# Attention with a relative bias, then a feed-forward layer: a new order for batch 0, other places for the q and k copies, 28 instead of 32 FFN matmuls per head pair

## The chip, the cores and the metric

The kernel runs on one core of a Trainium2 chip. The time is the device time of one execution in microseconds (us). A core has five engines with a queue of instructions each, worked off in order: TensorE (matmuls; its weight loads overlap them), VectorE, ScalarE, GpSimd and SyncE. They wait for each other through semaphores. Matmuls write to PSUM, a small memory of eight banks; VectorE and ScalarE read them from there. Transfers between the chip's main memory and the on-chip SBUF are issued here by GpSimd (loads) and SyncE (stores, transposing copies).

## The reference

Eight batches of eight heads, 576 rows, head size 64. The bias depends on the distance of two rows alone (32 buckets, the last from distance 128 on). The output of the attention, laid out as 4608 tokens of 512 numbers, goes through two matrix products with a leaky ReLU between them.

```python
scores = scale * np.matmul(q, k.transpose(0, 1, 3, 2))
scores = scores + bias.transpose(2, 0, 1)[None, :, :, :]
attn = np.exp(scores - np.max(scores, axis=-1, keepdims=True))
attn = attn / (np.sum(attn, axis=-1, keepdims=True) + 1e-09)
x = np.matmul(attn, v)            # then (batch, row) x (head, d): 4608 x 512
h = x @ w_in                      # 512 -> 2048
out = np.maximum(0.01 * h, h) @ w_out
```

## The kernel before

**Pairs.** The unit of the attention is a pair of heads `n` of 32 (four pairs `p` per batch `b`). Its steps are functions:

- `pair_rows(n)` (VectorE): copies the rows of q and k of two heads next to each other (tile `pr`).
- `transpose_q(n)`, `transpose_k(n)`: bring q and k to the form with the head dimension on the partitions (`qt`, `kt`). Up to pair 9 TensorE transposes into PSUM, from pair 10 on SyncE's transposing copy does it three pairs ahead (`turn_by_dma`, tile `tu`); a copy on VectorE or ScalarE writes `qt` and `kt`, and `apart` adds a form of the last 64 rows for both heads.
- `qk_mm(n, u)`: the scores, transposed, in six parts: `u` = 0 to 3 are four blocks of 128 key rows against the first 512 query rows (tile `ps_s`, two buffers of two banks), `u` = 4 is these blocks against the last 64 query rows (`ps_q`), `u` = 5 the last 64 key rows (`ps_s`).
- `exp(n, u, ps)` (ScalarE) writes the exponentials to `at` and `at4`, two buffers each by the parity of `n`.
- `band(n, u)` (VectorE) multiplies the diagonal band of the exponentials by the exponential of the bias, taken from tables `hk` and `hk4`. These are made at the start: row `ub` from the bias table, written to memory, and read back shifted by one per partition.
- `av_tails(n)`, `av(n, 0)`, `av(n, 1)`: value products of the last 64 key rows, then of the first and the second head (tile `ps_o`, one buffer, two banks, shared with `ps_q`). A column of ones in v gives the sum. After each `av`, VectorE takes the reciprocal and divides into `opair`.
- `x_transposes(n)`: `opair` to `xT`, by TensorE and a VectorE copy up to pair 5, for the last pair too, and by SyncE between.

**FFN.** Nine tiles of 512 tokens. An in-piece is four matmuls 128x512 and one activation on ScalarE (16 per tile), an out-piece four matmuls of an accumulation of 16 (16 per tile); after every fourth out-piece VectorE copies `y` and SyncE stores it. `moe(k)` does up to `k` in-pieces, `moe_block()` four out-pieces, or in-pieces if no out-piece is ready. A token tile is ready when its batches are finished (`finished`), and the in-pieces are at most two tiles ahead of the out-pieces. What is left after pair 32's step is done in `moe_rest()`, the tail. Pieces take their PSUM banks from a pool of two (`ps_m`, tag "m"), shared with transposes and in the tail joined by others.

**Order.** It is written by hand: each engine's instructions run in the program's order. The start warms TensorE with matmuls on zeros (`spin`), then pairs 0 and 1 are scored in a loop of their own (lines 531 to 545), with value products of pair 0 behind it. From pair 2 on a loop (line 553) does in turn: scores 0 and 1 of pair `n`, the value products of pair `n - 1` with an in-piece behind each, scores 2, 3, 4, `x_transposes(n - 1)`, the first half of the block, score 5, the q and k transposes and copies of pair `n + 1` (from pair 5 on), the second half of the block, two in-pieces.

Of the kernel before, what the change touches and what calls it, by code (L numbers as in the profile page):

```python
# [11 lines left out]
BF16 = mybir.dt.bfloat16  # L12
# [6 lines left out]
def bucket_runs(n_buckets, max_distance, seq):  # L19

    half = n_buckets // 2
    n = np.arange(seq)
    lr = np.log(np.maximum(n, 1).astype(np.float32) / half) / np.log(max_distance / half)
    large = np.minimum(half + (lr * (half - 1)).astype(np.int32), n_buckets - 1)
    bucket = np.where(n < half, n, large)
    assert (bucket[max_distance:] == n_buckets - 1).all()
    runs = []
    for d in range(max_distance):
        u = int(bucket[d])
        if runs and runs[-1][0] == u:  # L30
            runs[-1][2] = d
        else:
            runs.append([u, d, d])
    return runs
# [3 lines left out]
def kernel(  # L38
# [10 lines left out]
    nc = tc.nc  # L49
# [132 lines left out]
    C0 = 2 * P - 1  # L182
    small = NB // 2
    nc.vector.tensor_copy(out=ub[:, C0 : C0 + small], in_=e8[:, 0:small])
    for u, lo, hi in bucket_runs(NB, BAND, S):
        if lo >= small:
            nc.vector.tensor_copy(
                out=ub[:, C0 + lo : C0 + hi + 1],
                in_=e8[:, u : u + 1].to_broadcast([H, hi - lo + 1]),
            )  # L190
    row = ub[:, :]
    nc.vector.tensor_copy(
        out=ub[:, C0 - BAND + 1 : C0],
# [5 lines left out]
    def load_hk(h0, h1):  # L199
        nc.sync.dma_start(  # L200
            out=hk[:, h0:h1, :],
            in_=bass.AP(tensor=udr, offset=h0 * UW, ap=[[1, P], [UW, h1 - h0], [1, BW]]),
        )

    load_hk(0, 2)
    for e in range(2):
        nc.sync.dma_start(
            out=hk4[e * SL : (e + 1) * SL, :, :],
            in_=bass.AP(tensor=udr, offset=e * UW + SL + P, ap=[[1, SL], [2 * UW, n_pairs], [1, P + SL]]),
        )  # L210
    load_hk(2, H)

    def mirrored(t, lo, hi):

# [49 lines left out]
    def turned_pair(n, j):  # L264

        if by_dma(n):
            return turned[n][:, j * NC : (j + 1) * NC, :].rearrange("p c r -> p r c")
        if n <= n_pairs:
            ps = ps_m_pool.tile([P, 8 * P], BF16, name="ps_t", tag="m")
        else:  # L270
            if j == 0:
                turned[n] = ps_o_pool.tile([P, 2, 8 * P], BF16, name="ps_tt", tag="o")
            ps = turned[n][:, j, :]
        for c in range(NC):
            nc.tensor.transpose(ps[:, c * RQ : (c + 1) * RQ], in_=prs[n][0:RQ, j, c, :],
                                identity=ident[0:RQ, 0:RQ])
        return ps[:, 0:S].rearrange("p (c r) -> p r c", c=NC)
# [7 lines left out]

    def transpose_q(n):
        qt = qts[n] = qt_pool.tile([P, S], BF16, name="qt")
        copy = nc.scalar.copy if n <= n_pairs and n != 1 else nc.vector.tensor_copy
        copy(out=qt[:, 0:S].rearrange("p (r c) -> p r c", c=NC), in_=turned_pair(n, 0))  # L289

    def transpose_k(n):
        kt = kts[n] = kts_[n % 2]
        nc.vector.tensor_copy(out=kt[:, 0:S].rearrange("p (r c) -> p r c", c=NC), in_=turned_pair(n, 1))  # L293
        apart(kt)

    def qk_mm(n, u):

        qt, kt = qts[n], kts[n]
        if u == NJ:
            ps = ps_o_pool.tile([P, 2, 512], FP32, name="ps_q", tag="o")  # L300
            for c in range(NJ):
                for e in range(2):
                    r = slice(e * D, (e + 1) * D)
                    nc.tensor.matmul(ps[:, e, c * SL : (c + 1) * SL], lhsT=kt[r, c * P : (c + 1) * P],
                                     rhs=qt[r, 512:S], start=True, stop=True)
            return ps
        ps = ps_s_pool.tile([P, 2, 512], FP32, name="ps_s")
        if u < NJ:
            for e in range(2):
                r = slice(e * D, (e + 1) * D)  # L310
                nc.tensor.matmul(ps[:, e, :], lhsT=kt[r, u * P : (u + 1) * P], rhs=qt[r, 0:512],  # L311
                                 start=True, stop=True)
        else:
            nc.tensor.matmul(ps[:, 0, :], lhsT=kt[:, S : S + P], rhs=qt[:, 0:512], start=True, stop=True)
            nc.tensor.matmul(ps[:, 1, 0:SL], lhsT=kt[:, S : S + P], rhs=qt[:, 512:S], start=True, stop=True)  # L315
        return ps
# [4 lines left out]
    def exp(n, u, ps):  # L321
        at, at4 = at_view(n), at4_[n % 2]
        if u < NJ:
            nc.scalar.activation(at[:, :, u, 0:512], ps, AF.Exp, scale=scale)  # L324
        elif u == NJ:
            nc.scalar.activation(at[:, :, :, 512:S],  # L326
                                 ps[:, :, 0 : NJ * SL].rearrange("p e (c i) -> p e c i", i=SL),
                                 AF.Exp, scale=scale)
        else:
            nc.scalar.activation(at4[:, 0:S], ps.rearrange("p e i -> p (e i)")[:, 0:S], AF.Exp, scale=scale)  # L330
# [166 lines left out]
    def spin(k):  # L497
        pw = ps_m_pool.tile([P, 512], FP32, name="ps_w", tag="m")
        for _ in range(k):
            nc.tensor.matmul(pw, lhsT=junk[:, 0:P], rhs=junk, start=True, stop=True)  # L500

    def bands(n):
        for u in range(NJ + 2):
            band(n, u)

    spin(11)

    pair_rows(0)
    transpose_k(0)
    transpose_q(0)  # L510
    spin(5)
    def begin(n):
        b, p = items[n]
        if n == 0:
            load_w_in(0)
            load_v(1, 0, H, False)
            load_w_in(1)
            load_w_out(0)
            load_w_out(1)
        elif 0 < b < B - 1:  # L520
            if p < 2:
                load_qk(b + 1, 4 * p, 4 * p + 4)
            if p > 0:
                load_v_part(b + 1, p - 1)
        if n + 1 < N and not by_dma(n + 1):
            pair_rows(n + 1)
        if n + AHEAD < N and by_dma(n + AHEAD):
            pair_rows(n + AHEAD)
            turn_by_dma(n + AHEAD)

    for n in range(2):
        begin(n)
        ps_a, ps_b = qk_mm(n, 0), qk_mm(n, 1)
        exp(n, 0, ps_a)
        exp(n, 1, ps_b)
        transpose_q(n + 1)
        spin(3)
        ps_a, ps_b, ps_c = qk_mm(n, 2), qk_mm(n, 3), qk_mm(n, 4)
        exp(n, 2, ps_a)
        exp(n, 3, ps_b)  # L540
        transpose_k(n + 1)
        spin(4 - n)
        ps_a = qk_mm(n, 5)
        exp(n, 4, ps_c)
        exp(n, 5, ps_a)
    bands(0)
    av_tails(0)
    av(0, 0)
    av(0, 1)
    x_transposes(0)  # L550
    bands(1)

    for n in range(2, N + 1):
        live = n < N
        early = n + 1 <= n_pairs
        if x_by_dma(n - 2):
            finished(n - 2)
        if live:
            begin(n)
            ps_a, ps_b = qk_mm(n, 0), qk_mm(n, 1)  # L560
            exp(n, 0, ps_a)
            exp(n, 1, ps_b)
        av_tails(n - 1)
        av(n - 1, 0)
        if live:
            band(n, 0)
        if early:
            transpose_q(n + 1)
        moe(1)
        av(n - 1, 1)  # L570
        if live:
            band(n, 1)
        if early:
            transpose_k(n + 1)
        moe(1)
        if live:
            ps_a, ps_b, ps_c = qk_mm(n, 2), qk_mm(n, 3), qk_mm(n, 4)
            exp(n, 2, ps_a)
            band(n, 2)
            exp(n, 3, ps_b)  # L580
            exp(n, 4, ps_c)
            band(n, 4)
        x_transposes(n - 1)
        if not x_by_dma(n - 1):
            finished(n - 1)
        block = moe_block()
        next(block)
        if live:
            ps_a = qk_mm(n, 5)
            exp(n, 5, ps_a)  # L590
            band(n, 5)
        if n + 1 < N and not early:
            transpose_q(n + 1)
            transpose_k(n + 1)
        next(block)
        moe(2)
    moe_rest()


# [28 lines left out]
```

## Time and profile before

| what | us |
|---|---|
| median of 3 runs (428.47 to 433.93) | 429.24 |
| the profiled execution | 429.74 |
| its span, first to last instruction | 428.0 |
| TensorE busy | 376.7 |
| ScalarE busy | 239.5 |
| VectorE busy | 200.2 |
| GpSimd busy | 67.8 |

The mean granted TensorE clock of the profiled execution is 0.976 of full speed. Matmuls are pipelined, and a matmul's shown end is modelled, so the distance of two starts says more than the shown duration. In the timeline rows the columns are start, duration, engine, line, operation, output <- inputs, form, count, and in brackets the idle time of the engine before it with what ended it. In the rows of waits they are who waited for whom, us in total, times, and the longest. A few per cent of the matmul records are missing, so counts such as x3 or x7 stand for 4 or 8.

### The profile page before, as it was taken

To read this page: it belongs to the slowest core of one execution; us is meant where nothing else is said; L and a number is where in the kernel's file an instruction comes from. 1 tells how busy PE (TensorE), PEld (TensorE's weight loads), DVE (VectorE), ACT (ScalarE), POOL (GpSimd) and SP (SyncE) were. 2 spreads that over 40 slices of the span, in tenths; PEclk is the share of its full clock that TensorE was granted. 3 is DMA by queue.
4 is the path that set the end of the run, shared out by engine and by line. 5 is a ranking of instruction groups with operands and counts; after the bars stand their busy time and mean duration, and the time that the engine had idled before them with its cause. 6 is when DMAs were issued, how large, how long until landed. Compare 5 with 4: busy or idle time off the path is not lost.

```text
span 428.0 us, 8434 instructions
## 1 busy us (share of the span) xinstructions
PE 376.7 (88%) x3458; PEld 191.6 (45%) x3512; DVE 200.2 (47%) x517; ACT 239.5 (56%) x343; POOL 67.8 (16%) x98
## 2 busy tenths in 40 slices
PE   7777688778995999979999999999999999999995
PEld 2454344444443444444444444444444444444442
DVE  5457444665555555555555555555555520010121
ACT  3728475555686666666666666666666626316000
POOL 8734321015002400330042004000000000000000
PEclk9959899999998999999999999999999999999999
DMA  9999993149822984595479536943411100010111
GB/s 106 190 198 193 205 150 57 47 74 163 145 40 47 174 142 66 84 168 98 69 94 177 101 69 91 101 70 69 69 41 41 41 26 25 26 74 0 51 74 74
DMA packets 103613, 39.90 MB, mean 93 GB/s; under 512 B 82576, under 2 KB 97944, under 8 KB 103576
## 3 DMA queue, kind: packets, MB, share of 16 engines
q0 software_dynamic: 53664, 18.36, 41.9%
q1 hardware_dynamic: 49912, 21.02, 23.8%
q8 instruction: 27, 0.44, 0.4%
q14 instruction: 10, 0.08, 0.1%
HBM read 37.68 MB, written 9.45 MB: 110 GB/s over the span
## 4 chain that ended last, share of the span: by engine, by line
PE 55%; DVE 20%; ACT 15%; issue 7%; DMA 1%; another core or an unknown queue 1%; ACTq 0%; POOL 0%; POOLq 0%
PE pm L415 21%; PE pm L426 15%; PE ps_o L370 11%; ACT at L324 8%; DVE at L346 5%; PE ps_s L311 5%; ACT at L330 3%; DVE opair L374 3%; DVE y L431 3%; DVE qt L289 3%; DVE kt L293 3%; ACT at L326 3%; DVE rcp L373 1%; PE ps_o L359 1%; ACT gt L417 1%
## 5 line engine op out<-in xcount | busy, mean ns | idle before, releaser
L415 PE MATMUL pm<-xT,w_in_sb 128*128 128x512 bf16 x546 | 138.4, 379 | 14.8 <-DVE y L431 9.4
L417 ACT ACTIVATE gt<-pm 128x512 bf16<-128x512 f32 x144 | 86.2, 602 | 114.6 <-PE pm L415 114.5
L324 ACT ACTIVATE at<-ps_s 128x1024 bf16<-128x1024 f32 x128 | 124.0, 1027 | 34.0 <-PE ps_s L311 34.0
L426 PE MATMUL pm<-w_out_sb,gt 128*128 128x512 bf16 x553 | 130.7, 380 | 1.9 <-issue 0.7
L346 DVE TENSOR_TENSOR at<-at,hk 128x768 bf16<-128x768 bf16 (+3 forms) x160 | 72.0, 454 | 66.1 <-ACT at L324 30.5
L415 PEld LDWEIGHTS <-w_in_sb 128*128 128x128 bf16 x576 | 52.5, 98 | 71.4 <-issue 19.3
L426 PEld LDWEIGHTS <-gt 128*128 128x128 bf16 x576 | 53.0, 98 | 61.2 <-issue 1.0
L370 PE MATMUL ps_o<-vn,at 128*128 128x65 bf16 x1280 | 52.6, 198 | 5.5 <-DVE opair L374 5.5
L431 DVE COPY y<-pm 128x512 f32<-128x512 f32 x36 | 24.7, 687 | 69.1 <-PE pm L426 66.1
L370 PEld LDWEIGHTS <-at 128*128 128x128 bf16 x1280 | 47.3, 101 | 16.7 <-issue 11.9
L311 PE MATMUL ps_s<-qt,kt 64*128 64x512 bf16 x256 | 41.4, 396 | 10.3 <-DVE kt L293 7.0
L119 POOL DMA_DIRECT2D vn<-in_v_dram x24 | 21.1, 891 | 173.4 <-PE ps_o L370 168.7
L373 DVE RECIPROCAL rcp<-ps_o 128x5 f32<-128x5 f32 x64 | 12.5, 195 | 73.0 <-PE ps_o L370 72.8
L374 DVE TENSOR_TENSOR opair<-ps_o,rcp 128x320 bf16<-128x320 f32 x64 | 31.5, 491 | 2.2
L311 PEld LDWEIGHTS <-kt 64*128 64x128 bf16 x256 | 8.0, 95 | 36.0 <-issue 26.5
L330 ACT ACTIVATE at<-ps_s 128x576 bf16<-128x576 f32 x32 | 21.8, 681 | 1.7 <-PE ps_s L315 1.6
L326 ACT ACTIVATE at<-ps_q 128x512 bf16<-128x512 f32 x32 | 19.7, 617 | 0.0
L359 PEld LDWEIGHTS <-at 64*128 64x128 bf16 x320 | 9.5, 95 | 11.3 <-DVE at L346 2.5
L293 DVE COPY kt<-tu 128x576 bf16<-128x576 bf16 x22 | 14.3, 651 | 0.0
L289 DVE COPY qt<-tu 128x576 bf16<-128x576 bf16 x22 | 14.2, 647 | 0.0
L111 POOL DMA_DIRECT2D qn<-in_q_dram x17 | 12.0, 706 | 12.7 <-DVE pr L254 10.0
L359 PE MATMUL ps_o<-v,at 64*128 64x65 bf16 x320 | 11.1, 193 | 3.0 <-DVE at L346 1.9
(53 smaller groups left out, 165.7 us busy)
## 6 DMA issues: line engine op xcount, KB each, us to landing
out_dram<-y SPq DMA_DIRECT2D x36, 256.0 KB, 2.2
vn<-in_v_dram POOLq DMA_DIRECT2D x28, 128.0 KB, 5.4
qn<-in_q_dram POOLq DMA_DIRECT2D x12, 288.0 KB, 7.2
kn<-in_k_dram POOLq DMA_DIRECT2D x12, 288.0 KB, 7.9
w_in_sb<-in_moe_w_in_dram POOLq DMA_DIRECT2D x2, 1024.0 KB, 14.8
w_out_sb<-in_moe_w_out_dram POOLq DMA_DIRECT2D x2, 1024.0 KB, 16.0
qn<-in_q_dram POOLq DMA_DIRECT2D x4, 144.0 KB, 4.2
kn<-in_k_dram POOLq DMA_DIRECT2D x4, 144.0 KB, 4.5
```

The lines of the kernel that those rows point to most:

```text
L293: nc.vector.tensor_copy(out=kt[:, 0:S].rearrange("p (r c) -> p r c", c=NC), in_=turned_pair(n, 1))
L311: nc.tensor.matmul(ps[:, e, :], lhsT=kt[r, u * P : (u + 1) * P], rhs=qt[r, 0:512], start=True, stop=True)
L324: nc.scalar.activation(at[:, :, u, 0:512], ps, AF.Exp, scale=scale)
L326: nc.scalar.activation(at[:, :, :, 512:S], ps[:, :, 0 : NJ * SL].rearrange("p e (c i) -> p e c i", i=SL), AF.Exp, scale=scale)
L330: nc.scalar.activation(at4[:, 0:S], ps.rearrange("p e i -> p (e i)")[:, 0:S], AF.Exp, scale=scale)
L346: nc.vector.tensor_tensor(out=o, in0=o, in1=m, op=ALU.mult)
L370: nc.tensor.matmul(ps[:, ic, :], lhsT=at[:, o : o + P], rhs=vn[b % NBUF][:, c, 2 * p + e, :], start=False, stop=(ic == NJ and c == NJ - 1))
L374: nc.vector.tensor_tensor(out=opair[:, :, e * D : (e + 1) * D], in0=ps[:, :, 0:D], in1=rcp.to_broadcast([P, NJ + 1, D]), op=ALU.mult)
L415: nc.tensor.matmul(pm, lhsT=w_in_sb[:, c, f * P : (f + 1) * P], rhs=xT[c][:, t0 : t0 + TT], start=(c == 0), stop=(c == n_cc - 1))
L417: nc.scalar.activation(gt[:, f, :], pm, AF.Prelu, bias=0.0, scale=1.0, alpha=0.01)
L426: nc.tensor.matmul(pm, lhsT=gt[:, f, ts * P : (ts + 1) * P], rhs=w_out_sb[:, f, :], start=(f == 0), stop=(f == n_fc - 1))
L431: nc.vector.tensor_copy(out=y, in_=pm)
```

## The change

The row `ub` of the bias is made with fewer copies: neighbouring runs of equal width share one, and every third goes to ScalarE. The table `hk` of heads 2 and 3 gets a transfer of its own. Batch 0 (pairs 0 to 3) is written out by itself, and so is pair 4: each score is followed by its exponential at once, the next pair's scores 0 and 1 come ahead of the present pair's end, scores stand between and ahead of the value products, part 5 comes before part 4, and bands are put behind their exponentials. From pair 5 on the q and k transposes and copies of the next pair move from behind score 5 to behind the first and the second value product, TensorE's transposes always use the pool "m", and the loop ends with one in-piece instead of two. The q copy of pair 1 goes to ScalarE.

```diff
     nc.vector.tensor_copy(out=ub[:, C0 : C0 + small], in_=e8[:, 0:small])
+    groups = []
     for u, lo, hi in bucket_runs(NB, BAND, S):
         if lo >= small:
-            nc.vector.tensor_copy(
-                out=ub[:, C0 + lo : C0 + hi + 1],
-                in_=e8[:, u : u + 1].to_broadcast([H, hi - lo + 1]),
-            )
+            w = hi - lo + 1
+            if groups and groups[-1][2] == w:
+                groups[-1][3] += 1
+            else:
+                groups.append([u, lo, w, 1])
+    for j, (u, lo, w, m) in enumerate(groups):
+        copy = nc.scalar.copy if j % 3 == 2 else nc.vector.tensor_copy
+        copy(out=ub[:, C0 + lo : C0 + lo + m * w].rearrange("h (m w) -> h m w", w=w),
+             in_=e8[:, u : u + m].unsqueeze(2).to_broadcast([H, m, w]))
...
     load_hk(0, 2)
+    load_hk(2, 4)
...
-    load_hk(2, H)
+    load_hk(4, H)
...
-        if n <= n_pairs:
-            ps = ps_m_pool.tile([P, 8 * P], BF16, name="ps_t", tag="m")
-        else:
-            if j == 0:
-                turned[n] = ps_o_pool.tile([P, 2, 8 * P], BF16, name="ps_tt", tag="o")
-            ps = turned[n][:, j, :]
+        ps = ps_m_pool.tile([P, 8 * P], BF16, name="ps_t", tag="m")
...
-        copy = nc.scalar.copy if n <= n_pairs and n != 1 else nc.vector.tensor_copy
+        copy = nc.scalar.copy if n <= n_pairs else nc.vector.tensor_copy
...
-        if n + 1 < N and not by_dma(n + 1):
+        if n_pairs < n + 1 < N and not by_dma(n + 1):
             pair_rows(n + 1)
...
-    for n in range(2):
-        begin(n)
-        ps_a, ps_b = qk_mm(n, 0), qk_mm(n, 1)
-        exp(n, 0, ps_a)
-        exp(n, 1, ps_b)
-        transpose_q(n + 1)
-        spin(3)
-        ps_a, ps_b, ps_c = qk_mm(n, 2), qk_mm(n, 3), qk_mm(n, 4)
-        exp(n, 2, ps_a)
-        exp(n, 3, ps_b)
-        transpose_k(n + 1)
-        spin(4 - n)
-        ps_a = qk_mm(n, 5)
-        exp(n, 4, ps_c)
-        exp(n, 5, ps_a)
-    bands(0)
-    av_tails(0)
-    av(0, 0)
-    av(0, 1)
-    x_transposes(0)
-    bands(1)
-
-    for n in range(2, N + 1):
+    def score(n, u):
+        exp(n, u, qk_mm(n, u))
...
+    pair_rows(1)
+    score(0, 0)
+    score(0, 1)
+    for n in range(n_pairs):
+        begin(n)
+        if n == 1:
+            bands(0)
+        elif n > 1:
+            band(n - 1, 5)
+            band(n - 1, 4)
+        if n < 3:
+            transpose_k(n + 1)
+        if n < 2:
+            spin(3)
+        score(n, 2)
+        if n > 0:
+            av_tails(n - 1)
+            av(n - 1, 0)
+            band(n, 0)
+        score(n, 3)
+        if n > 0:
+            band(n, 1)
+            av(n - 1, 1)
+        if n == 3:
+            pair_rows(n + 1)
+            transpose_k(n + 1)
+        transpose_q(n + 1)
+        if n < 1:
+            spin(3)
+        score(n, 5)
+        if n < 2:
+            pair_rows(n + 2)
+        if n > 0:
+            band(n, 2)
+        score(n, 4)
+        if n > 0:
+            x_transposes(n - 1)
+        score(n + 1, 0)
+        score(n + 1, 1)
+
+    n = n_pairs
+    begin(n)
+    band(n - 1, 5)
+    band(n - 1, 4)
+    av_tails(n - 1)
+    av(n - 1, 0)
+    av(n - 1, 1)
+    score(n, 2)
+    x_transposes(n - 1)
+    finished(n - 1)
+    band(n, 0)
+    band(n, 1)
+    transpose_k(n + 1)
+    moe(1)
+    score(n, 3)
+    band(n, 2)
+    transpose_q(n + 1)
+    moe(1)
+    score(n, 4)
+    band(n, 4)
+    moe(1)
+    score(n, 5)
+    band(n, 5)
+    moe(3)
+
+    for n in range(n_pairs + 1, N + 1):
         live = n < N
-        early = n + 1 <= n_pairs
+        more = n + 1 < N
...
-        if early:
+        if more:
             transpose_q(n + 1)
         moe(1)
         av(n - 1, 1)
         if live:
             band(n, 1)
-        if early:
+        if more:
             transpose_k(n + 1)
         moe(1)
...
-        if n + 1 < N and not early:
-            transpose_q(n + 1)
-            transpose_k(n + 1)
         next(block)
-        moe(2)
+        moe(1)
     moe_rest()
```

More of the change, by code (lines that the diff above doesn't have):

```diff
@@ L504, in bands @@
             band(n, u)
[L506 to L511, printed above, removed]
     def begin(n):
@@ L529, in begin @@
             turn_by_dma(n + AHEAD)
-    for n in range(2):
-        begin(n)
-        ps_a, ps_b = qk_mm(n, 0), qk_mm(n, 1)
-        exp(n, 0, ps_a)
-        exp(n, 1, ps_b)
-        transpose_q(n + 1)
-        spin(3)
-        ps_a, ps_b, ps_c = qk_mm(n, 2), qk_mm(n, 3), qk_mm(n, 4)
-        exp(n, 2, ps_a)
-        exp(n, 3, ps_b)
-        transpose_k(n + 1)
-        spin(4 - n)
-        ps_a = qk_mm(n, 5)
-        exp(n, 4, ps_c)
-        exp(n, 5, ps_a)
-    bands(0)
-    av_tails(0)
-    av(0, 0)
-    av(0, 1)
-    x_transposes(0)
-    bands(1)
-    for n in range(2, N + 1):
+    def score(n, u):
+        exp(n, u, qk_mm(n, u))
+    spin(11)
+    pair_rows(0)
+    transpose_k(0)
+    transpose_q(0)
+    spin(5)
+    pair_rows(1)
+    score(0, 0)
+    score(0, 1)
+    for n in range(n_pairs):
+        begin(n)
+        if n == 1:
[19 more added lines that the diff above has]
+            transpose_k(n + 1)
+        transpose_q(n + 1)
+        if n < 1:
[35 more added lines that the diff above has]
+    for n in range(n_pairs + 1, N + 1):
         live = n < N
-        early = n + 1 <= n_pairs
+        more = n + 1 < N
         if x_by_dma(n - 2):
```

## The prediction

> **What bounds the kernel now.** I read the page first (busy shares and slices), then the busy time by stage, then the timeline of single pairs, last the waits. The page's slices:
>
> ```profile
> span 428.0 us, 8434 instructions
> ...
> PE   7777688778995999979999999999999999999995
> ...
> PEclk9959899999998999999999999999999999999999
> ```
>
> The profiled run took 429.74 us, 1.74 more than its span and 0.1% above the median of 429.24, so I sum on the span and add 1.74. TensorE is full from the second third on, and only partly so in the first ten slices, where its clock also drops. The stages, by pair: batch 0 from the first scores to pair 4, and pairs 5 to 32.
>
> ```profile
> 8.52:40.27 31.75, 23.30 (x299) 14.69 (x300) 17.97 (x47) 20.06 (x26) 18.05 (x26) 0.78 1.48 188
> ...
> 56.02:352.78 296.76, 265.43 (x2706) 136.40 (x2751) 160.31 (x401) 187.90 (x267) 37.62 (x50) 0.99 0.67 89
> ```
>
> Columns after the length are busy us of TensorE, its weight loads, VectorE, ScalarE and GpSimd, then the clock. In batch 0 ScalarE has 20 of 32 us and nobody is full: that stage is chains. In the long stage only TensorE comes near the length. Here is pair 15, from its first scores to the next pair's, and pair 31, which differs in one thing: no pair follows whose q and k must be copied.
>
> ```profile
> 164.15 0.61 PE L311 MATMUL ps_s<-qt,kt 64*128 64x512 bf16 x4
> ...
> 172.35 1.03 PE L415 MATMUL pm<-xT,w_in_sb 128*128 128x512 bf16 x4
> ...
> 173.13 0.68 DVE L431 COPY y<-pm 128x512 f32<-128x512 f32 x1
> ...
> 173.87 1.02 PE L415 MATMUL pm<-xT,w_in_sb 128*128 128x512 bf16 x4 [0.49 <-DVE y L431]
> 174.83 0.39 PE L311 MATMUL ps_s<-qt,kt 64*128 64x512 bf16 x2
> ...
> 334.89 0.60 PE L311 MATMUL ps_s<-qt,kt 64*128 64x512 bf16 x4
> ...
> 343.09 1.97 PE L415 MATMUL pm<-xT,w_in_sb 128*128 128x512 bf16 x8
> 344.99 0.33 PE L359 MATMUL ps_o<-v,at 64*128 64x65 bf16 x10
> ```
>
> Pair 15 takes 10.68 us. Between its last two in-pieces TensorE waits for the copy of y, which stands on VectorE behind the copies of the next q and k. In pair 31 these copies are absent, the two pieces run as one, and the pair takes 10.10. The other waits of TensorE, over the whole run:
>
> ```profile
> PE pm L415 <- DVE y L431: 9.4, 18, 0.8
> ...
> PE ps_tt L275 <- DVE qt L289: 7.6, 5, 1.7
> PE ps_s L311 <- DVE kt L293: 7.0, 3, 3.2
> PE ps_o L370 <- DVE opair L374: 5.5, 7, 1.1
> ```
>
> **FFN pieces moved to the tail: nothing by itself.** A piece is four matmuls. The price of a matmul, and the two ends of the tail:
>
> ```profile
> 100.08 1.73 PE pm L426 x8
> ...
> 352.61 2.62 PE L415 MATMUL pm<-xT,w_in_sb 128*128 128x512 bf16 x11
> ...
> 423.69 0.69 DVE y L431
> ```
>
> 1.73 / 8 = 0.216 us, so a piece is 0.864. Counting pieces through the planner's rules (what is ready, at most two token tiles ahead), pairs 4 to 32 do 208 of the 288 pieces now and 188 afterwards; 20 pieces, 80 matmuls, 17.3 us, go to the tail. The tail begins when pair 32's two in-pieces end (352.61 + 1.73 = 354.34) and has 80 pieces: 69.1 us, to 423.4. It has no gaps, so it lengthens by 17.3 exactly, and the pairs shorten by 17.3 plus or minus what happens to their waits.
>
> **Pairs 5 to 32.** Work of a pair outside the FFN: 10.10 - 32 x 0.216 = 3.19. Now the stage lasts 354.34 - 56.02 = 298.3 us (pair 5's first scores are quoted below). Its work is 27 x 3.19 = 86.1, pair 32 outside the FFN 9.35 - 6.91 = 2.4, 202 pieces 174.5, and some 3.1 for transposes on TensorE in the first five pairs: 266.1. So 32 us are waits. I go through them.
>
> In the ordinary pair (3 in-pieces, 4 out-pieces; 19 pairs) the q and k copies now stand on VectorE behind the first and second division of the value products, ahead of nothing that TensorE wants soon: the next user of the bank that y leaves is the first in-piece of the next pair, one piece, four scores and twenty value matmuls later (about 2 us, against 0.68 for y). What is queued behind the q copy is the second reciprocal; it comes some 0.1 us late, and the waiter, the scores of the fifth key block, has about 0.3 us in hand. So these waits go: 18 of 0.66 (173.87 - 172.35 - 0.864), 11.9 us. The pair becomes 10.10 - 0.864 = 9.24.
>
> ```profile
> 56.02 0.60 PE L311 MATMUL ps_s<-qt,kt 64*128 64x512 bf16 x4
> ...
> 101.74 0.60 PE L311 MATMUL ps_s<-qt,kt 64*128 64x512 bf16 x4
> ...
> 181.57 1.12 ACT L417 ACTIVATE gt<-pm 128x512 bf16<-128x512 f32 x2
> ...
> 184.69 0.61 PE L311 MATMUL ps_s<-qt,kt 64*128 64x512 bf16 x4 [3.21 <-DVE kt L293]
> ```
>
> Pairs 5 to 8 take 45.7 us now with 22 pieces: work 4 x 3.19 + 19.0 + 2.6 = 34.4, waits 11.3. Afterwards their transposes pass through the in-pieces' banks, each followed by a piece or a value product, so the wait between the q and the k transposes goes. But pairs 7 and 8 have no in-piece to put between the value products, VectorE runs four row copies and the q copy ahead of the divisions, and pair 5 has seven in-pieces whose activations stand behind three exponentials. Following the new order with the durations above I keep about 7 of the 11.3.
>
> Pairs without an out-piece ready end now on the k copy (pair 16: 3.21). Afterwards the copy is early and the next scores wait for a score bank, that is for the exponential, behind the activations on ScalarE (the row at 181.57). I put 1.5 on each of pairs 11, 17 and 26 (7 in-pieces) and 2.4 on pairs 12 and 13 together: 6.9 in the place of 7.0 and of about 2 us of smaller waits. Waits after: 0 + 7.3 + 6.9 = 14.2 instead of 32.1. The pairs lose 17.3 + 17.9, the tail takes 17.3 back: **-17.9**.
>
> **Batch 0.** ScalarE's exponentials before:
>
> ```profile
> 8.95 3.77 ACT L324 ACTIVATE at<-ps_s 128x1024 bf16<-128x1024 f32 x4 [1.52 <-PE ps_s L311]
> ...
> 36.42 0.64 ACT L289 COPY qt<-ps_t 128x576 bf16<-128x576 bf16 x1
> 38.28 1.94 ACT L324 ACTIVATE at<-ps_s 128x1024 bf16<-128x1024 f32 x2 [1.22 <-PE ps_s L311]
> 40.10 0.60 ACT L326 ACTIVATE at<-ps_q 128x512 bf16<-128x512 f32 x1
> ...
> 41.11 1.97 ACT L324 ACTIVATE at<-ps_s 128x1024 bf16<-128x1024 f32 x2
> ```
>
> Pair 0 starts at 8.95, pair 4 at 41.11. In a row, two exponentials need 1.82 (38.28 to 40.10), the two small ones 1.01 (40.10 to 41.11), the q copy 0.64: 5.29 a pair. The new order issues each score ahead of value products and the next pair's first two scores ahead of the pair's end. Pair 0 then ends at 8.95 + 5.29 = 14.24. From pair 1 on, one gap of 0.4 remains: the second value product waits for the division of the first, the q transposes follow it, and ScalarE needs them. 14.24 + 3 x 5.7 = 31.3. Two things can push this out:
>
> ```profile
> 3.59 1.16 DVE L187 COPY ub<-e 8x3 bf16<-8x3 bf16 x15
> ...
> hk<-u_row SPq DMA_DIRECT2D x2, 96.0 KB, 6.1
> ...
> 29.27 1.26 PE L370 MATMUL ps_o<-vn,at 128*128 128x65 bf16 x20 [0.33 <-DVE opair L374]
> ...
> 36.89 0.77 PE L370 MATMUL ps_o<-vn,at 128*128 128x65 bf16 x20 [0.56 <-DVE opair L374]
> ...
> 36.00:38.00 2.00, 1.44 (x37) 1.22 (x35) 1.29 (x5) 1.03 (x2) 0.73 (x2) 1.00 1.14 213
> ...
> 43.58 1.26 PE L370 MATMUL ps_o<-vn,at 128*128 128x65 bf16 x20 [0.81 <-DVE opair L374]
> ...
> 44.00:46.00 2.00, 2.00 (x29) 1.07 (x27) 1.09 (x3) 0.58 (x1) 1.03 (x2) 0.50 1.24 209
> ```
>
> The band's last part lands 6.1 us after its issue; 11 copies, 8 of them on VectorE, instead of 15 bring that forward by some 0.5 us, and the extra transfer for heads 2 and 3 goes ahead of it. The first value product still meets it: 0.6. And at clock 0.50 twenty value matmuls take 1.26 instead of 0.77; with the transposes that is 1.3 a pair. At 36 to 38 the same work in 6.7 us a pair kept clock 1.00; by 43.58, where TensorE had been waiting more, it had fallen. I charge one pair of three: 31.3 + 0.6 + 1.3 = 33.2, that is 7.9 before 41.11. The Trainium skill (TensorE: Matmul & The Clock Gate, section Why this matters for your kernels) asks for no idle gaps over about 3 us between bursts, else half clock. This trace does not agree: the longest gap between 41 and 44 is 0.81 us, and the clock still fell.
>
> Pair 4 does 6 in-pieces before and after. From its first exponential to pair 5's scores it takes 56.02 - 41.11 = 14.9; in the new order (value products before its own third score, transposes between the pieces) I count 11.9, with TensorE held about 1.5 us by VectorE copies: -3.0. Weights must be there:
>
> ```profile
> 27.60 0.75 POOL L232 DMA_DIRECT2D w_in_sb<-in_moe_w_in_dram  x1 [2.26 <-DMA kn<-in_k_dram]
> ...
> w_in_sb<-in_moe_w_in_dram POOLq DMA_DIRECT2D x2, 1024.0 KB, 14.8
> ```
>
> The second half lands at about 42.4; its first user is pair 5's third in-piece, near 50. The queue of loads is not moved in batch 0. So batch 0 and pair 4: **-10.9**, between -5 (all at half clock, loads late) and -13.5 (never at half clock, no wait for the band).
>
> Sum: 428.0 - 10.9 - 17.9 = 399.2, plus 1.74: **401 us**.
>
> **Rivals.** *The clock holds* (the page's rule): no pair of batch 0 runs at half clock, 401 - 1.3 = 399.7. For: TensorE gets denser. Against: the fall at 43. Chance 0.2. *Half clock through batch 0*: two more pairs and pair 4, +3.6: 404.5; 0.1. *The wait moves inside the pair*: the q and k copies between the divisions hold the fifth block's scores and the second value product by as much as y did, 19 x 0.66 = 12.5: 413.5. For: the slack is only 0.3 us. Against: VectorE is busy for little over half of this stage. Chance 0.13. *The pair is a latency chain, not TensorE's work*: pair 16 did 16 FFN matmuls and still took 9.86 us (174.83 to 184.69). Then a pair stays at 10.68 with 28, and the tail's 17.3 are paid for nothing: 429.7 - 10.9 + 17.3 = 436, slower. It is slower than before once a pair stays above about 10.3. Against: that pair ended on the k copy, which moves. Chance 0.07, a little over half of it beyond 2% with batch 0 earning less. That the change does not do what it says is small: the order is written by hand and each engine's instruction order follows it.
>
> **Numbers.** Forecast 0.45, the four rivals 0.5, 0.05 for the rest, spread about no change. A measurement here tells about 2% (8.6 us) from no change: under 420.7 is faster. Faster 0.87, same 0.08, slower 0.05. Range 391 (half of the kept 14 us of waits gone as well, and the clock holding) to 414 (the moved wait).
>
> **What will show it.** Pair 4's first exponential near 33 us, pair 5's first scores near 45; ordinary pairs at 9.2 with no wait for y; the tail near 88 us long; the clock in the windows of 15 to 33 us. Wrong would be: ordinary pairs over 9.6, or waits of TensorE for the opair or qt copies in each of them, or batch 0 waiting for loads.

## The result and the profile after

The changed kernel takes 400.21 us (median of 4 runs, 398.67 to 401.78), the kernel before 431.18 in the same comparison (4 runs): ratio 0.928, 95% interval 0.920 to 0.937. The forecast was 401. The total is right, but two of its terms are off by about 5 us each, in opposite directions; the rest of this document is about those two.

The profiled execution took 401.34 us. Its page, to set beside the one of before:

```profile
span 399.2 us, 8424 instructions
...
PE 372.1 (93%) x3456; PEld 190.7 (48%) x3508; DVE 200.9 (50%) x509; ACT 239.5 (60%) x347; POOL 68.9 (17%) x98
...
PE   7776989889998999999999999999999999999995
...
PEclk9997799899999999999999999999999999999999
```

TensorE was busy 376.7 of 428.0 us before and 372.1 of 399.2 now: of the 28.8 us its busy time gave 4.6, its gaps the other 24.2. What it waited for, over the whole run (the five largest):

```profile
PE pm L417 <- ACT gt L419: 3.8, 4, 1.5
PE ps_o L372 <- DVE opair L376: 3.7, 6, 0.8
PE ps_s L313 <- ACT at L326: 2.8, 5, 1.0
PE ps_s L313 <- ACT at L332: 2.4, 3, 1.1
PE ps_t L277 <- DVE pr L261: 2.1, 2, 1.7
```

Columns: who waited for whom, us in total, times, longest. The three largest waits of before (y 9.4, the q copy 7.6, the k copy 7.0) are gone from the list; further down, 0.5 us for a q copy and 0.6 for a k copy are left, at the start and in batch 0. The busy time by stage shows where the 28.8 us of the span came from: first scores to pair 4, pair 4, pairs 5 to 32, tail.

```profile
8.17:35.00 26.83, 19.39 (x294) 12.26 (x294) 18.25 (x47) 20.79 (x27) 16.13 (x24) 0.94 1.56 189
35.00:50.12 15.12, 13.53 (x110) 7.11 (x109) 7.80 (x21) 8.62 (x13) 5.31 (x7) 0.66 1.23 208
50.12:308.55 258.43, 247.25 (x2636) 129.90 (x2678) 160.61 (x400) 180.31 (x256) 40.45 (x53) 0.99 0.85 104
308.55:399.20 90.65, 85.98 (x393) 39.05 (x399) 9.70 (x15) 26.88 (x45) 0.00 (x0) 1.00 0.12 44
```

The number after the ScalarE and GpSimd columns is the granted clock. Up to pair 5's first scores (56.02 before, 50.12 now) 5.9 us were won; pairs 5 to 32 went from 298.3 to 258.4, 39.9 less; the tail from 428.0 - 354.34 = 73.7 to 90.65, 17.0 more. 5.9 + 39.9 - 17.0 = 28.8. The forecast had 10.9, 17.9 + 17.3 = 35.2, and 17.3: the same 28.8. So batch 0 and pair 4 gave 5.0 less, the long stage 4.7 more, and the tail took 0.3 less.

An ordinary pair of the long stage on TensorE, from its first scores to the next pair's, and the copies of VectorE beside it:

```profile
96.96 0.60 PE L313 MATMUL ps_s<-qt,kt 64*128 64x512 bf16 x4
...
101.24 0.28 PE L306 MATMUL ps_q<-qt,kt 64*128 64x64 bf16 x8
...
105.17 1.03 PE L417 MATMUL pm<-xT,w_in_sb 128*128 128x512 bf16 x4
106.12 0.61 PE L313 MATMUL ps_s<-qt,kt 64*128 64x512 bf16 x4
```

```profile
99.43 0.66 DVE L291 COPY qt<-tu 128x576 bf16<-128x576 bf16 x1
...
100.27 0.49 DVE L376 TENSOR_TENSOR opair<-ps_o,rcp 128x320 bf16<-128x320 f32 x1
...
105.37 0.69 DVE L433 COPY y<-pm 128x512 f32<-128x512 f32 x1 [0.71 <-PE pm L428]
```

The pair takes 9.16 us and has no bracket on TensorE. The y copy starts as soon as its matmuls end. The q copy delays the second division, which ends at 100.76, but its waiter (the row at 101.24) comes 0.48 us later: the slack on which the third rival turned is there, and it suffices.

Batch 0 is another matter. ScalarE sets its pace, and these are its idle times there with the row that follows each, then the pair 4 rows:

```profile
17.84 1.02 ACT L326 ACTIVATE at<-ps_s 128x1024 bf16<-128x1024 f32 x1 [1.14 <-PE ps_s L313]
20.12 0.64 ACT L291 COPY qt<-ps_t 128x576 bf16<-128x576 bf16 x1 [1.25 <-PE ps_t L277]
...
26.13 0.64 ACT L291 COPY qt<-ps_t 128x576 bf16<-128x576 bf16 x1 [0.49 <-PE ps_t L277]
...
34.13 0.64 ACT L291 COPY qt<-ps_t 128x576 bf16<-128x576 bf16 x1 [2.65 <-PE ps_t L277]
...
35.68 1.96 ACT L326 ACTIVATE at<-ps_s 128x1024 bf16<-128x1024 f32 x2
40.59 1.02 ACT L326 ACTIVATE at<-ps_s 128x1024 bf16<-128x1024 f32 x1 [2.94 <-PE ps_s L313]
```

Behind the 1.14 and the 2.65 stand these two rows, the second with the VectorE work that it waited for:

```profile
16.21 0.26 DVE L348 TENSOR_TENSOR at<-at,hk 128x192 bf16<-128x192 bf16 x1 [1.74 <-DMA hk<-u_row]
...
30.07 0.20 DVE L375 RECIPROCAL rcp<-ps_o 128x5 f32<-128x5 f32 x1 [1.74 <-PE ps_o L372]
...
32.29 0.74 DVE L261 COPY pr<-qn 96x768 bf16<-96x768 bf16 x1
32.96 0.34 DVE L261 COPY pr<-kn 96x768 bf16<-96x768 bf16 x1
```

```profile
33.35 0.68 PE L277 MATMUL ps_t<-ident,pr 96*128 96x96 bf16 x12 [1.74 <-DVE pr L261]
...
36.65 1.28 PE L372 MATMUL ps_o<-vn,at 128*128 128x65 bf16 x20
```

The band of pair 0 waits for its table until 16.21. In pair 3 the row copies of pair 4 stand on VectorE behind both divisions, so TensorE waits 1.74 us to transpose them, though VectorE itself was idle for 1.74 us before 30.07. And from 35.16 to 45.40 us TensorE runs at half clock: the twenty value matmuls at 36.65 take 1.28 us.

### The profile page after: what moved, and what is told of

It is laid out like the page before. It is cut to its first block, busy times and chain, and to the rows that moved or that the text cites. A ratio compares the mean times of both kernels' runs of the same rounds, so it can differ in the third digit from the quotient of the medians.

```text
span 399.2 us, 8424 instructions
## 1 busy us (share of the span) xinstructions
PE 372.1 (93%) x3456; PEld 190.7 (48%) x3508; DVE 200.9 (50%) x509; ACT 239.5 (60%) x347; POOL 68.9 (17%) x98
## 4 chain that ended last, share of the span: by engine, by line
PE 79%; DVE 9%; ACT 4%; issue 3%; DMA 3%; another core or an unknown queue 1%; SPq 0%; ACTq 0%; DVEq 0%
PE pm L428 31%; PE pm L417 27%; PE ps_o L372 10%; PE ps_s L313 7%; DVE opair L376 2%; ACT at L326 2%; DVE at L348 2%; DMA hk<-u_row 2%; PE ps_s L316 1%; PE ps_o L361 1%; DVE rcp L375 1%; DVE qt L291 1%; DVE pr L261 1%; PE ps_q L306 1%
## 5 line engine op out<-in xcount | busy, mean ns | idle before, releaser
L428 PE MATMUL pm<-w_out_sb,gt 128*128 128x512 bf16 x560 | 132.1, 380 | 1.3 <-ACT gt L419 0.3
L372 PE MATMUL ps_o<-vn,at 128*128 128x65 bf16 x1280 | 51.6, 197 | 3.7 <-DVE opair L376 3.7
L119 POOL DMA_DIRECT2D vn<-in_v_dram x24 | 22.2, 932 | 147.2 <-PE ps_o L372 137.3
L295 DVE COPY kt<-tu 128x576 bf16<-128x576 bf16 x22 | 14.2, 646 | 0.0
L316 PE MATMUL ps_s<-qt,kt 128*128 128x512 bf16 x32 | 12.4, 387 | 0.0
## 6 DMA issues: line engine op xcount, KB each, us to landing
w_in_sb<-in_moe_w_in_dram POOLq DMA_DIRECT2D x2, 1024.0 KB, 14.2
w_out_sb<-in_moe_w_out_dram POOLq DMA_DIRECT2D x2, 1024.0 KB, 16.9
```

What stands on the lines that cost most here:

```text
L119: nc.gpsimd.dma_start(out=vn[i][:, c, :, 0:D], in_=v[b, :, c * P : (c + 1) * P, :].rearrange("h s d -> s h d"),)
L372: nc.tensor.matmul(ps[:, ic, :], lhsT=at[:, o : o + P], rhs=vn[b % NBUF][:, c, 2 * p + e, :], start=False, stop=(ic == NJ and c == NJ - 1))
L428: nc.tensor.matmul(pm, lhsT=gt[:, f, ts * P : (ts + 1) * P], rhs=w_out_sb[:, f, :], start=(f == 0), stop=(f == n_fc - 1))
```

## The experiments

The kernel before had medians of 433.38, 431.71 and 433.30 us in the three comparisons (experiments 1 to 4, 5 to 8, 9 and 10). Ratios are to these.

**1. One in-piece less, and nothing else.** On the kernel before, at the end of the loop from pair 2 on. Is the wait for y gone because the copies of q and k moved, or because the bank that y leaves is wanted later?

```diff
-        moe(2)
+        moe(1)
```

> The kernel before with one in-piece instead of two at the end of each pair, all else as it was. Theory A (the wait for y goes because the copies of the next q and k move away from ahead of it; a piece less only moves work to the tail): the ordinary pair loses its piece alone, 0.86, and keeps 0.4 to 0.7 of wait in another place, now for the k copy, since that ends at 173.2 in the trace of before and the next scores would want it at 173.3; the time stays within 424 to 430. Theory B (the piece that goes is the one that met the wait; the next user of y's bank then stands about 2 us later, whatever the copies do): the 18 waits for y go, 11.9 us, the k copy holds at most 0.1 a pair: 417 to 420.

Measured: 420.94 us (418.68 to 421.10), ratio 0.972 (0.966 to 0.979), 0.9 us above theory B's range and well below theory A's. The wait for y is gone. One pair, and the VectorE copies behind it:

```profile
236.57 0.61 PE L311 MATMUL ps_s<-qt,kt 64*128 64x512 bf16 x4
...
245.73 0.61 PE L311 MATMUL ps_s<-qt,kt 64*128 64x512 bf16 x4
...
247.04 1.03 PE L415 MATMUL pm<-xT,w_in_sb 128*128 128x512 bf16 x3
```

```profile
244.74 0.64 DVE L293 COPY kt<-tu 128x576 bf16<-128x576 bf16 x1
...
245.56 0.68 DVE L431 COPY y<-pm 128x512 f32<-128x512 f32 x1
```

The y copy still stands behind the q and k copies (the row at 244.74 is k's) and ends at 246.24, as late as ever. The next in-piece in need of a bank comes at 247.04. The pair is at 9.16 us, the changed kernel's period. The waits for the q and k copies in the early pairs and in pairs without an out-piece stay (7.9 and 4.3 us in this run's waits).

**2. The copies moved, and nothing else.** On the kernel before, q and k transposes and copies behind the first and second value product from pair 2 on, always with pool "m"; two in-pieces at the end of the loop as before.

```diff
-        if early:
+        if more:
             transpose_q(n + 1)
...
-        if early:
+        if more:
             transpose_k(n + 1)
...
-        if n + 1 < N and not early:
-            transpose_q(n + 1)
-            transpose_k(n + 1)
```

> The kernel before with the q and k transposes and copies behind the first and second value product as in the change, two in-pieces at the end kept, batch 0 as before. Theory A: y is copied as soon as its last matmul is done, 0.9 us later it has left its bank, one piece (0.86) covers it, the ordinary pair takes 10.1 as pair 31 did; with the k-copy waits and the transposes of pairs 5 to 8 the loop gives 17 to 22 us: 408 to 413. Theory B (28 matmuls are what counts): the wait for y stays in half of its size, 0.3 a pair, 414 to 419.

Measured: 403.55 us (403.08 to 403.91), ratio 0.933 (0.927 to 0.939): 29.8 us of the change's 31.0 with no new batch 0 and no piece dropped. The ordinary pair:

```profile
238.41 0.60 PE L306 MATMUL ps_s<-qt,kt 64*128 64x512 bf16 x4
...
246.63 1.97 PE L410 MATMUL pm<-xT,w_in_sb 128*128 128x512 bf16 x8
248.53 0.61 PE L306 MATMUL ps_s<-qt,kt 64*128 64x512 bf16 x4
```

10.12 us with 32 FFN matmuls, the two last in-pieces as one run of eight, no wait for y. That is 0.96 more than 9.16, for a piece of 0.864, so the fourth in-piece costs little beyond its matmuls. The time is 4.5 us under the lower end of theory A, and part of that is in pair 4: this row is that pair, from its first exponential to pair 5's scores.

```profile
41.08:53.19 12.11, 9.56 (x106) 5.18 (x108) 6.94 (x20) 7.90 (x12) 2.77 (x4) 1.00 1.26 206
```

It took 14.9 us before, with windows at clock 0.50, and 12.11 here at 1.00.

**3. The new batch 0 alone.** The changed kernel with the old loop: copies behind score 5, two in-pieces, the old pool for transposes from pair 6 on.

```diff
-        if more:
-            transpose_q(n + 1)
         moe(1)
...
-        if more:
-            transpose_k(n + 1)
         moe(1)
...
+        if more:
+            transpose_q(n + 1)
+            transpose_k(n + 1)
         next(block)
-        moe(1)
+        moe(2)
```

> The changed kernel with the old end of the pair from pair 5 on (copies behind score 5, two in-pieces, transposes of pairs 6 to 9 in the value products' banks): the new start alone. If the parts add up: 429.7 - 5.9 (pair 5 starts at 50.1 instead of 56.0) = 424. If the loads or the FFN take the start's gain back later: 427 to 430. By my own sum on record, -10.9: 419.

Measured: 425.55 us (424.68 to 426.64), ratio 0.984 (0.978 to 0.991). In its waits the one for y is back:

```profile
PE pm L422 <- DVE y L438: 9.2, 18, 0.7
```

That is 7.8 us of medians, and less than the 2% that the forecast takes as the limit of a measurement, so by the times alone the result is unclear. Its pair 5 starts at 50.42, like the changed kernel's, 5.6 us earlier than before. Part of the 7.8 is the clock: runs at a mean of 0.975 to 0.980 took 429.46 and 429.60 us with the kernel before, and 424.68 and 424.94 with this one.

**4. The changed kernel with two in-pieces.** 32 matmuls per pair, everything else as changed.

```diff
-        moe(1)
+        moe(2)
```

> The changed kernel with two in-pieces at the end of a pair again (32 matmuls), all else changed. Theory A: the count is worth nothing by itself; the ordinary pair 10.1, the tail shorter by as much: 400 to 403. Theory B: a wait for y of about 0.3 comes back in 19 pairs: 405 to 408.

Measured: 398.45 us (397.14 to 400.60), ratio 0.922 (0.914 to 0.930), below theory A's range and far from theory B's; its interval overlaps the changed kernel's. Its pair takes 10.12 us and has no wait for y. With the copies moved the number of pieces is worth nothing, as the forecast's first step says. In its profile the clock stood at 1.00 in pair 4, and pair 5 began at 47.03 rather than 50.12, which accounts for more than the difference of the two. From experiment 2 to this one only the new start is added, and it gives 403.55 - 398.45 = 5.1 us, the clock's part included. So the parts do not simply add up: experiments 2 and 3, 29.8 and 7.8 us, make 37.6, and both together 34.9. Both shorten pair 4. The clock raised the next question.

**5 to 8. What holds batch 0.** Four edits of the changed kernel. (The expectations call the row copies "row additions", the table `hk4` the four-row mask and `hk` the two-row one. Only the second transfer of `hk` changes places.) The first puts pair 4's row copies where VectorE is idle:

```diff
         elif n > 1:
             band(n - 1, 5)
             band(n - 1, 4)
+        if n == 3:
+            pair_rows(n + 1)
...
         if n == 3:
-            pair_rows(n + 1)
             transpose_k(n + 1)
```

> The changed kernel with one move: in pair 3 of batch 0 the three row additions that pair 4's key transposes wait for go to VectorE right behind bands 5 and 4 (where VectorE is idle from 28.3 to 30.1 us) instead of behind the second division, for which TensorE waited 1.74 us. Theory A (this gap is also what lets the granted clock fall to 0.50 from 35 us): pair 4's first exponential about 1.5 us earlier, no window at 0.50 between 34 and 44, pair 5's first scores at 46 to 47 instead of 50.1, time 396 to 397. Theory B (the wait is a delay and nothing else, the clock falls anyway): pair 5's first scores at 48.5 to 49, time 398.5 to 399. Theory C (ScalarE or the band multiplications set the pace there, so that the wait only moves): no difference, 400.

The second leaves these copies and fills TensorE's gap:

```diff
             pair_rows(n + 1)
+            spin(6)
             transpose_k(n + 1)
```

> The changed kernel with six matmuls on zeros (512 columns, 0.216 us each at full clock) put into TensorE's queue in pair 3 just ahead of pair 4's key transposes: the wait for the row additions stays, but TensorE is busy through 1.3 us of it. Theory A (the fall of the clock at 35 us comes from TensorE's low busy share in pair 3): the windows from 36 to 44 us stay near 1.00, pair 4 takes 11.5 us instead of 14.4, pair 5's first scores at 47, time 397 to 398. Theory B (the clock falls on its own schedule, or the fall costs nothing): the windows show 0.50 in them or pair 4 stays at 14 us, time 399.5 to 400.5.

The third moves one transfer behind those of `hk4`:

```diff
     load_hk(0, 2)
-    load_hk(2, 4)
...
+    load_hk(2, 4)
     load_hk(4, H)
```

(the two transfers of `hk4` stand where the three dots are).

> The changed kernel with the two transfers of the four-row window mask issued ahead of the two of the two-row one on the sync queue. Theory A (the landing of the second part at 16.16 us is set by its place in the queue): it is issued about 0.9 us earlier and lands 0.5 to 0.9 us earlier, the second half of pair 0's tail product waits that much less, pair 4's first exponential comes 0.5 to 1 us earlier, time 399 to 399.7. Theory B (the landing is set by the traffic of the other loads): it lands within 0.2 us of 16.16, time unchanged at 400.2, or up to 1 us more as bands 5 and 4 of pair 0 then wait for the two-row mask.

The fourth has all three, with `spin(4)` for `spin(6)`.

> The changed kernel with all three: row additions of pair 4 early, four-row mask first, and four matmuls on zeros (0.86 us at full clock) in TensorE's queue ahead of pair 4's key transposes. If delay and clock fall both go: pair 5's first scores at 46 us and 395.5 to 397. If the clock falls all the same, the gain is the two delays alone less the 0.86 us of added matmuls: 398.5 to 400.

Measured, in us (ratio with its interval; the last three columns from each profile, so from one execution: first scores to pair 4's first exponential, from there to pair 5's first scores, and the stretches in which the clock was 0.50):

| kernel | median (range) | ratio | to pair 4 | pair 4 | half clock from, to |
|---|---|---|---|---|---|
| changed | 400.21 (398.67 to 401.78) | 0.928 (0.920 to 0.937) | 27.51 | 14.44 | 18.1 to 21.5, 35.2 to 45.4, 72.7 to 76.1 |
| 4: two pieces | 398.45 (397.14 to 400.60) | 0.922 (0.914 to 0.930) | 26.39 | 12.20 | 117.2 to 120.6 |
| 5: rows early | 397.33 (395.51 to 400.13) | 0.921 (0.916 to 0.926) | 26.33 | 14.14 | 19.4 to 22.8, 36.5 to 43.3, 121.8 to 125.2 |
| 6: gap filled | 399.20 (395.96 to 400.03) | 0.922 (0.917 to 0.928) | 26.60 | 13.52 | 40.6 to 44.1, 71.4 to 74.8 |
| 7: hk4 first | 398.65 (396.81 to 400.15) | 0.923 (0.918 to 0.928) | 26.10 | 12.14 | none |
| 8: all three | 397.11 (394.86 to 398.28) | 0.919 (0.914 to 0.923) | 24.58 | 12.23 | none |
| 9: changed again | 400.96 (396.91 to 401.97) | 0.927 (0.921 to 0.933) | 27.65 | 11.81 | 18.7 to 22.1, 121.1 to 124.5 |
| 10: more filled | 396.65 (395.32 to 397.25) | 0.918 (0.913 to 0.922) | 25.01 | 11.93 | none |

Experiment 5 took the wait away. Its key transposes, at once behind the value products:

```profile
31.66 0.77 PE L372 MATMUL ps_o<-vn,at 128*128 128x65 bf16 x20 [0.49 <-DVE opair L376]
32.26 0.68 PE L277 MATMUL ps_t<-ident,pr 96*128 96x96 bf16 x12
```

The way to pair 4 became 27.51 - 26.33 = 1.2 us shorter, with a fall of the clock near 20 us in both. The clock then fell again all the same, so a fall does not need the 1.74-us gap. Whether the gap makes one likelier, one profile cannot say, and this one is of the slowest of six runs: their mean clocks are 0.983 to 0.999, against 0.979 to 0.995 in ten runs of the changed kernel, and the median, 397.33, lies between theories A and B. In experiment 6's profile a fall came at 40.6 us in spite of the added matmuls; its median lies between its two theories, and of its time nothing certain can be said. Experiment 7's median is under both of its theories, but its profile is of its fastest run, at clock 1.00, and the five others are at 0.987 to 0.995. In that profile the wait moved. The bands of pair 0 on VectorE:

```profile
14.82 1.93 DVE L348 TENSOR_TENSOR at<-at,hk 128x512 bf16<-128x512 bf16 x5 [3.30 <-DMA hk<-u_row]
```

All in a row, so `hk4` is there in time, but the first part of `hk`, which the swap does not move, landed at 14.82, against 11.91 in the changed kernel's profile. With the swap (experiments 7, 8 and 10) pair 0's last band ended at 16.8, 15.3 and 16.0 us, without it (the changed kernel, experiments 4 to 6 and 9) at 16.5, 16.9, 17.3, 17.3 and 16.8. So the swap may be worth up to 1 us, but these landings scatter by more than that between executions, and the time alone (26.10 against 26.39 to pair 4, neither with a fall of the clock) decides nothing. Experiment 8's 24.58 is 1.8 us under experiment 4's 26.39, neither with a fall by then; how that splits between the early row copies, the swap and a luckier landing stays open. Its median, 397.11, is 0.1 us above what it expected with both delays and the fall gone.

**9 and 10. The clock by itself.** The changed kernel once more, and experiment 8 with matmuls on zeros in pair 4 as well:

```diff
+    spin(3)
     av_tails(n - 1)
     av(n - 1, 0)
+    spin(3)
     av(n - 1, 1)
     score(n, 2)
```

> The changed kernel as it is, run again, to separate what the clock costs from what the order costs. Theory A (the fall of the granted clock differs between executions of one program and costs about 3.3 us when it comes twice, at 20 and at 36 to 44 us): the runs spread over some 4 us and the span falls with the mean granted clock, from about 399.5 at 0.979 to about 394.5 at 1.00; in a profile in which the windows from 18 to 46 us show 1.00, pair 4's first exponential comes at 34.5 and pair 5's first scores at 46.8 to 47. Theory B (the clock only follows from this program's gaps): the clock is 0.979 to 0.991 in every run and pair 5's first scores come at 50 again.

> The kernel with the three edits together, and three matmuls on zeros (0.65 us at full clock) each ahead of the tail products of pair 3 and between its two value products, where TensorE stood 0.72 and 0.81 us before. Theory A (the fall of the clock at 36 us comes from TensorE's low busy share there): a mean granted clock of 0.996 or more in every run, and a smaller spread than the 3.4 us of the version without them, 394.5 to 396. Theory B (the fall does not depend on these gaps): the clock still is 0.991 in some of the runs, the spread stays, and the added 1.3 us of matmuls cost 0 to 1 us: 397 to 398.

The same program with the same order, in two executions. The first fence is the profile of the changed kernel shown above, the second that of its repetition, both by windows of 2 us:

```profile
36.00:38.00 2.00, 1.72 (x30) 1.35 (x27) 0.80 (x4) 1.64 (x2) 1.41 (x3) 0.50 1.12 211
38.00:40.00 2.00, 1.25 (x22) 1.16 (x21) 0.66 (x2) 0.00 (x0) 0.59 (x1) 0.50 1.20 212
```

```profile
35.18:47.67 12.49, 10.37 (x111) 5.30 (x111) 7.71 (x21) 8.56 (x13) 5.01 (x7) 1.00 1.21 208
18.00:20.00 2.00, 1.51 (x27) 1.48 (x26) 1.46 (x5) 1.02 (x1) 0.77 (x1) 0.67 1.84 175
20.00:22.00 2.00, 2.00 (x21) 1.08 (x21) 1.97 (x6) 1.59 (x3) 1.76 (x2) 0.50 1.36 199
36.00:38.00 2.00, 1.21 (x30) 0.94 (x30) 1.33 (x6) 1.82 (x2) 1.52 (x3) 1.00 1.12 211
38.00:40.00 2.00, 1.14 (x23) 0.79 (x23) 0.99 (x3) 0.50 (x1) 1.14 (x2) 1.00 1.18 207
```

In the repetition the clock held through pair 4 (column of 0.50 against 1.00), and pair 5 began at 47.67, not 50.12. Over its six runs the span follows the mean granted clock: 399.4 and 399.8 us at 0.979, 398.4 and 399.2 at 0.983, 396.9 at 0.991, 394.8 at 0.995. That is theory A in its slope, with a spread of 5.1 us; the first fall, near 20 us, was there in both profiles, so the profile that A foresaw at 1.00 throughout was not seen.

Why it differs, the kept traces show better than the times. In each of the twelve profiles every change of the clock lies a whole number of 3.41 us from the first one: in the changed kernel at 4.44, 18.09, 21.50, 35.16, 45.40, 72.70 and 76.12 us, in the repetition at 5.04, 18.70, 22.11, 121.10 and 124.51. So each execution is cut into windows of 3.41 us, and where the cuts lie differs between executions. The windows around pair 3's wait, in the changed kernel and in the repetition:

```profile
31.74:35.16 3.42, 1.68 (x29) 1.27 (x30) 2.83 (x7) 1.03 (x2) 1.95 (x3) 1.00 2.15 168
```

```profile
32.35:35.76 3.41, 2.11 (x31) 1.36 (x32) 2.85 (x7) 1.46 (x3) 2.27 (x3) 1.00 1.91 179
```

In the first TensorE is busy for 0.49 of the window and the fall follows; in the second for 0.62, and none does. Over the twelve profiles, the tail's last 12 us left out, there are 24 falls. Of the windows at full clock in which TensorE was busy for less than 0.50, 11 of 14 were followed by one, between 0.50 and 0.66 it was 13 of 71, and above that none of 1220. What decides in the middle range is not shown.

Experiment 10 is at 0.995 to 1.00 in all six runs, with a spread of 1.9 us, against 0.991 to 1.00 and 3.4 us without the added matmuls, and costs nothing that can be seen: 396.65 against 397.11. That is theory A's clock to within 0.001, but the time is 0.65 us above A's range and below B's. One window at half clock lowers the mean by 0.5 x 3.41 / 394 = 0.004, so the five runs at 0.995 or 0.996 have room for one fall each. Where it came, their runs do not say; both profiles of the changed kernel had one behind pair 4 (72.70 and 121.10), where nothing was added. All this speaks for TensorE's low busy share in a window as the cause of a fall; six runs each don't prove the remedy. This version is 1.1% under the changed kernel measured beside it (396.65 against 400.96), and its runs, 395.32 to 397.25, lie below all but one of that kernel's.

## Why the prediction was right, and where not

The total came within 1 us, and that is partly luck: batch 0 with pair 4 was put 5.0 us too favourably, the long stage 4.7 too cautiously, and the two cancel. The mechanism of the larger part, the waits that go, held.

**Pieces moved: nothing by itself.** Right. The tail grew by 17.0 us against 17.3, and experiment 4, with the pieces put back, has the same time within its interval. The forecast's last list is off from its own terms here: "near 88 us" should be 73.7 + 17.3 = 91.0, and 90.65 was measured. Its lower bound for batch 0, -13.5, is also 0.7 more than the terms it names (10.9 + 1.3 + 0.6 = 12.8).

**The ordinary pair.** Right in size, 9.16 against 9.24. The forecast gave the y wait one cure with two parts: copies that are no longer ahead of y, and a next user of y's bank that comes 2 us later. Experiments 1 and 2 show that each of these alone is enough. In the changed kernel only one was needed.

**The other pairs of the long stage.** Here lies the first wrong term, the sum of 14.2 us of waits left after. These are TensorE's waits in the changed kernel from 50.12 to 308.55 us:

```profile
PE pm L417 <- ACT gt L419: 3.8, 4, 1.5
PE ps_s L313 <- ACT at L332: 2.3, 2, 1.1
PE ps_o L372 <- DVE opair L376: 1.4, 2, 0.8
PE ps_s L313 <- ACT at L326: 0.8, 2, 0.5
...
```

With two small ones left out here, 0.3 and 0.2, they add up to 8.8. The kinds are those that the forecast names (in-pieces behind their activations, scores behind exponentials, value products behind a division); the sizes were put too high, 1.5 us for each pair with seven in-pieces where pairs 11, 17 and 26 wait 0.76, and 7.3 for pairs 5 to 8 where their brackets sum to 4.5. 14.2 - 8.8 is 5.4 us, and 19 ordinary pairs at 0.08 less make 1.5 more; the stage was only 4.7 shorter than forecast. The fall of the clock from 72.70 to 76.12, which the forecast does not have, goes the other way; how the remaining 2.2 us split I can't say.

**Batch 0.** The second wrong term: pair 4's first exponential came at 35.68 instead of 33.2. The forecast had a gap of 0.4 for ScalarE in each pair from 1 on, 0.6 for the band and 1.3 for one pair at half clock, 3.1 in all. ScalarE's idle times above are 1.14 (the band), 1.25 (pair 1's q copy at half clock), 0.49 and 2.65: 5.5. So the step that failed is "one gap of 0.4 remains", in pair 3 alone. The change leaves the row copies of pair 4 behind the second division, and the forecast counted for the q transposes the division of the first product only. Experiment 5 gives back 1.2 us of it. The charge of one pair at half clock, 1.3, was about right in that profile: experiment 4, the same program up to there, took 1.1 us less without the fall.

**Pair 4.** Forecast 11.9, measured 14.44. The order is right: at clock 1.00 it takes 11.8 to 12.2 in five profiles of the table. I had charged half clock to one pair of batch 0 and none to pair 4; in the profiled execution that was 2.2 to 2.6 us (14.44 against 12.20 in experiment 4 and 11.81 in the repetition). This was a rival's condition ("half clock through batch 0"), which came half true.

**The rivals.** The moved wait and the latency chain are refuted by the 9.16 us pair without a bracket. The clock is not one case or the other: it differs between executions of one program, with the place of the 3.41-us windows, so "the clock holds" was a coin and not a mechanism of this change. The page's rule behind that rival (the Trainium skill, TensorE: Matmul & The Clock Gate, section Why this matters for your kernels) fails here a second time: TensorE's longest wait for another engine in the changed kernel's list is 1.7 us, and the clock fell to 0.50. The same page of the Trainium skill (section What's actually happening) states that the activity window is free-running and does not start with the kernel. The traces agree: the clock's first change came at 4.44 us in one execution and at 5.04 in the other, and all later ones at whole numbers of 3.41 us from it.

## What to carry to other kernels

A wait for a copy that frees a bank has two cures, an earlier copy or a later next user; look for the cheaper, and don't count both. When a stage is rewritten by hand, go through every engine's queue once for each unit, the last unit of the stage too: the forecast took the steady step for pair 3, whose row copies stand elsewhere. Where a stage is a chain in which TensorE is busy for only half or two thirds, give its time as two values, with the clock and without, because one profiled execution shows only one of them.

## What the runs showed of the hardware

The granted clock fell to 0.50 for 3.4 to 10.2 us at a time in profiles of the changed kernel and its variants in which TensorE's longest wait for another engine was 1.5 to 1.9 us, and at different places in two executions of the same program. Within an execution its changes lie 3.41 us or a multiple apart, and all 24 falls follow a window of that length in which TensorE was busy for at most 0.66 of it. For the whole kernel this was worth up to 5 us between runs (394.8 us of span at a mean clock of 0.995, 399.8 at 0.979), more than several of the edits tested here. With TensorE's gaps in pairs 3 and 4 filled with matmuls on zeros, the mean stayed at 0.995 or above in six runs of six, which leaves room for at most one fall in each.
